# Scores as 64x64 quarters, q copied in one piece, the second batch's keys turned ahead of the MLP's second product

## The chip, the cores and the metric

The kernel runs on one core of a Trainium2 chip. The core has a matrix engine (TensorE, PE in the profile; its weight loads are listed as PEld), a vector engine (VectorE, DVE), an activation engine (ScalarE, ACT), a general engine (GpSimd, POOL) and a queue engine that issues DMAs (SyncE, SP). The metric is the device time in microseconds (us) of one execution. The time before is the median of three runs.

## The reference

Three stages follow each other. Everything is float32.

```python
# attention: q, k, v are (2, 8, 768, 64); block 32, window 16
k_sum = k.reshape(B, H, nb, block, D).max(axis=3)
v_sum = v.reshape(B, H, nb, block, D).mean(axis=3)
scores_l = where(|pos_q - pos_k| < window, scale * q @ k.T, -1e9)
scores_s = scale * q @ k_sum.T + log(block)
a = softmax(concat([scores_l, scores_s]))
x = a @ concat([v, v_sum])              # then to 1536 tokens x 512
# MLP: w_in (512, 2048), w_out (2048, 512)
h = x @ w_in;  x = (h * sigmoid(h)) @ w_out
# mixture of 8 experts, top 1, capacity 384: w1 (8, 512, 1024), w2 (8, 1024, 512)
e = argmax(x @ w_gate); out = gate * (relu(x @ w1[e]) @ w2[e])
```

## The kernel before

Attention works in 24 units. A unit is 256 queries (four blocks of 64) of a pair of heads; twelve units make a batch of the input, and four units with the same queries make one block `xT` of 256 tokens for the MLP. The main loop calls `attn_step(n)` for n from -2 on, and a step holds pieces of several units: the scores `s_mm` of unit n, the row minimum `s_max`, exponential `s_exp` and normalization `s_norm` of unit n-1, the turn of the probabilities `p_mm`/`p_ev` of unit n-2, the product with the values `a_mm` and its copies `x_hi`/`x_lo` of unit n-3, and the queries' turn `q_mm`/`q_ev` of unit n+1. From step 7 on a step also holds one MLP step s = n-7: `l1(s)`, twelve matmuls of 256 columns for one slice f of 128 hidden columns, `g_mul`, `g_hi`, `g_lo`, and `l2` of the step two before, six matmuls of 512 columns. There are 96 MLP steps; after the attention they go on alone, and the experts follow. The order in which the code calls the functions is the order on each engine; nothing is reordered later, and each engine works its instructions off one after the other.

The keys of a head pair are prepared by `k_prep(b, p)`: six transposes on PE into two PSUM banks kA and kB, copies by ACT of twelve overlapping windows of 96 keys into `kwin`, and the maxima of 32 keys by DVE (`ks`), which go behind each window as 24 more columns. A `k_prep` runs in steps -1 to 2 for the first batch and in steps 11 to 14 for the second one ("k steps" below), near the end of the step, after `l2`. The scores multiply a 128x128 stationary matrix `qbd`, in which the two heads' queries stand as a block diagonal (the rest is zero, set once by POOL), with the 120 columns of a window: four float32 matmuls for a unit, each of which the trace shows as two records. `q_ev` fills `qbd` by four ACT copies.

The block means of the values come in the first batch from PE (`vsum_mm`, six matmuls, called at the end of step 0; ACT copies the result), in the second batch from POOL and DVE (`vs_reduce`) with eight small DMAs (`vs_place`). `vs_rows` is the DMA that puts them under the values of each unit.

The MLP's weights W0, W1, ... are loaded raw as pairs `ri`, `ro` and turned into two float32r parts by `conv`: per half three DVE operations (`cv`), an ACT cast and a POOL subtraction. `conv_part` takes the next DVE operation of the queue, three of them in a step; `conv_until` forces what an `l1` needs. All attention tiles in PSUM share four buffers of the tag `att`.

## Time and profile before

| | |
|---|---|
| median of three runs | 515.15 us (514.3 to 515.69) |
| the profiled execution | 514.7 us, its span 513.0 us |
| busy share of the span | PE 94%, PEld 81%, DVE 58%, ACT 48%, POOL 26% |
| granted TensorE clock, mean | 0.976 of full speed |

The span runs from the first instruction to the last one in the trace. PE's share is an average: in the first four of 40 slices of the span the page shows it at 4 to 8 tenths, and in nearly all later ones at 9. A DVE, ACT or POOL that waits while PE is busy costs nothing.

### The profile page before, as it was taken

The page shows a single profiled execution, that of the slowest core. Times are in us where ns is not written, and L with a number is a line of the kernel's source. Part 1 is how long each engine was busy: PE and PEld are TensorE (multiplying, and loading weights), DVE is VectorE, ACT ScalarE, POOL GpSimd, SP SyncE. Part 2 cuts the span into 40 slices and gives each one's busy share as a digit, 9 for nine tenths or more (in the row PEclk, how much of TensorE's full clock was granted, in tenths as well). Part 3 has the DMA queues.
Part 4 walks back from the last instruction along what each step waited for, and adds up shares of the span by engine and source line. Part 5 has one row for each costly group of instructions (what it writes and reads, how often), then busy time and mean ns, then how long its engine had stood idle before and what let it go on. Part 6 is the DMA issues. An engine that isn't in the chain of part 4 may idle for free. (4 is left out here: it accounts for less than half of the span.)

```text
span 513.0 us, 9798 instructions
## 1 busy us (share of the span) xinstructions
PE 479.9 (94%) x3318; PEld 416.8 (81%) x3318; DVE 296.0 (58%) x857; ACT 247.4 (48%) x746; POOL 135.6 (26%) x154
## 2 busy tenths in 40 slices
PE   4877989999999999999999999999999998999994
PEld 2366878898988899999998998888878897988852
DVE  1277886765545988666666434556666673445500
ACT  4478868977753533333333333334543344346511
POOL 6027753362433532222112100112412012101011
PEclk9957989999999999999999999999999999999998
DMA  8479777246301677655540000128251367718470
GB/s 204 101 201 278 187 193 200 65 121 165 75 2 42 173 211 215 217 156 149 151 177 0 1 1 0 44 74 318 78 191 55 89 204 226 251 45 288 151 236 16
DMA packets 82055, 71.15 MB, mean 139 GB/s; under 512 B 36822, under 2 KB 66776, under 8 KB 81984
## 3 DMA queue, kind: packets, MB, share of 16 engines
q1 hardware_dynamic: 80288, 66.17, 44.6%
q0 software_dynamic: 1696, 4.13, 2.1%
q8 instruction: 33, 0.54, 0.4%
q14 instruction: 38, 0.31, 0.2%
HBM read 55.38 MB, written 15.09 MB: 137 GB/s over the span
## 5 line engine op out<-in xcount | busy, mean ns | idle before, releaser
L451 PE MATMUL hp<-xT,w 128*128 128x256 f32 x1152 | 156.8, 286 | 2.3 <-ACT w L436 1.4
L451 PEld LDWEIGHTS hp<-xT,w 128*128 128x128 f32 x1152 | 149.6, 192 | 8.1 <-ACT w L436 1.6
L481 PE MATMUL x<-w,g 128*128 128x512 f32 x576 | 151.6, 398 | 1.1 <-ACT rows L487 1.1
L481 PEld LDWEIGHTS x<-w,g 128*128 128x128 f32 x576 | 101.8, 189 | 20.2 <-issue 2.1
L454 ACT ACTIVATE u<-hp 128x256 f32<-128x256 f32 x96 | 37.0, 385 | 98.3 <-PE hp L451 94.8
L459 DVE SCALAR_TENSOR_TENSOR u<-u,hp 128x256 f32<-128x256 f32 x96 | 40.2, 418 | 63.9 <-ACT u L454 63.6
L463 ACT CAST g<-u 128x256 fp32r<-128x256 f32 x96 | 39.4, 410 | 60.3 <-DVE u L459 60.0
L437 POOL TENSOR_TENSOR w<-cv,w 128x512 fp32r<-128x512 f32 x32 | 42.8, 1339 | 95.9 <-ACT w L436 95.8
L791 PE MATMUL hp<-XT,H 128*128 128x384 f32 (+1 forms) x288 | 48.8, 320 | 2.2 <-ACTq L948 1.4
L791 PEld LDWEIGHTS hp<-XT,H 128*128 128x128 f32 x288 | 45.8, 188 | 4.6 <-ACTq L948 1.8
L757 PE MATMUL y<-H,gh 128*128 128x512 f32 x192 | 48.6, 397 | 0.0
L467 DVE TENSOR_TENSOR g<-u,g 128x256 fp32r<-128x256 f32 x72 | 31.4, 437 | 27.6 <-ACT g L463 17.0
L326 POOL TENSOR_TENSOR P<-P,rs 128x480 f32<-128x480 f32 x24 | 26.3, 1095 | 60.6 <-DVE rs L325 53.8
L757 PEld LDWEIGHTS y<-H,gh 128*128 128x128 f32 x192 | 35.1, 188 | 7.2 <-issue 0.4
L736 DVE TENSOR_TENSOR H<-R,H 128x1024 fp32r<-128x1024 f32 x24 | 29.4, 1224 | 17.2 <-ACT H L735 17.2
L568 POOL DMA_INDIRECT disp<-rows,di x12 | 13.4, 1119 | 97.5 <-DVE rows L566 58.7
L316 ACT ACTIVATE P<-P,nm 128x120 f32<-128x120 f32 x96 | 36.6, 384 | 4.2 <-DVE nm L305 4.1
L796 ACT ACTIVATE gh<-hp 128x384 fp32r<-128x384 f32 (+1 forms) x24 | 10.9, 456 | 47.2 <-PE hp L791 46.7
L294 PEld LDWEIGHTS sc<-kwin,qbd 128*128 128x128 f32 x192 | 28.3, 220 | 4.8 <-DVE nm L305 1.7
L294 PE MATMUL sc<-kwin,qbd 128*128 128x120 f32 x192 | 30.2, 308 | 2.0 <-DVE nm L305 1.0
L735 ACT CAST H<-R 128x1024 fp32r<-128x1024 f32 x27 | 28.1, 1042 | 2.2 <-SPq L948 1.6
L765 POOL DMA_INDIRECT out_dram<-ys,aux x8 | 9.8, 1231 | 72.2 <-ACT ys L764 36.5
(175 smaller groups left out, 576.7 us busy)
## 6 DMA issues: line engine op xcount, KB each, us to landing
R<-in_moe_w_dram SPq DMA_DIRECT2D x34, 512.0 KB
ri<-in_moe_w_in_dram SPq DMA_DIRECT2D x16, 512.0 KB
ro<-in_moe_w_out_dram SPq DMA_DIRECT2D x16, 512.0 KB
disp<-zt SPq DMA_DIRECT2D x24, 260.0 KB
q_n<-in_q_dram SPq DMA_DIRECT2D x48, 64.0 KB
k_n<-in_k_dram SPq DMA_DIRECT2D x16, 192.0 KB
out_dram<-zt SPq DMA_DIRECT2D x12, 256.0 KB
rows<-in_moe_w_dram SPq DMA_DIRECT2D x6, 512.0 KB
```

What stands on the lines that cost most here:

```text
L294: PE.matmul(sc[:, i, :], lhsT=qbd[u % 2][:, i, :], rhs=kwin[p][:, i0 + i, :], start=True, stop=True)
L316: ACT.activation(P[:, i, :], P[:, i, :], AF.Exp, bias=nm[:, i : i + 1], scale=-1.0, accum_out=sm[:, i : i + 1])
L437: POOL.tensor_sub(w[:, 2 * j + 1, :], t, w[:, 2 * j, :].bitcast(F32))
L451: PE.matmul(hp, lhsT=w[:, a, c], rhs=x[:, b_, kk, :], start=n == 0, stop=n == 3 * KT - 1)
L454: ACT.activation(u, hp, AF.Tanh, scale=0.5)
L459: DVE.scalar_tensor_tensor(out=u, in0=u, scalar=1.0, in1=hp_t.pop(s), op0=ALU.add, op1=ALU.mult)
L463: ACT.copy(gt[s][:, 0, :], u_t[s])
L467: eng.tensor_sub(gt[s][:, 1, :], u_t.pop(s), gt[s][:, 0, :].bitcast(F32))
L481: PE.matmul(x2[blk][t], lhsT=gh[:, a, c], rhs=w[:, b_, :], start=first and n == 0, stop=last and n == 2)
L736: (eng or DVE).tensor_sub(h[:, 1], r, h[:, 0].bitcast(F32))
L757: PE.matmul(y, lhsT=gh[:, a, c], rhs=mx[1, f // 2][:, b_, DM * (f % 2) : DM * (f % 2) + DM], start=first and n == 0, stop=last and n == 2,)
L791: PE.matmul(hp, lhsT=h1(f // 2, a, kk, c), rhs=XT[:, b_, kk, 0:N], start=n == 0, stop=n == 3 * KT - 1)
```

## The change

The scores: `qbd` is gone. `q_mm` turns the queries into a tile `qa` that stays allocated in one `att` buffer (its other half takes `a_mm`'s result), `q_ev` copies all 256 columns at once, and `s_mm` issues eight matmuls with a 64x64 stationary matrix: head h picks the rows of the array, the parity e of the query block its columns. Each head writes a PSUM tile of its own. The mask has three patterns instead of six. The q loads give each partition two pieces of 256 bytes, where it was one of 512.

The keys: kB takes seven instead of six transposes with kA together, so that no window is cut and four ACT copies do for eight. The first batch's kA and kB lie in the tag `x2`. The second batch's `k_prep` is called after `q_mm` and before `l2`.

The order: `vsum_mm` is called at the end of step 1 instead of 0, into the tag `h`, and DVE copies its result. `vs_rows` is called a step later (for unit n-2) and behind `l2`, `vs_place` a step later. W0 and W1 enter the conversion queue in steps 3 and 5 instead of 2 and 4. Constants that only the routing uses are made after the mask.

```diff
+    qa = psum.tile([128, 2, 256], F32, tag="att", bufs=4, name="qa")
...
-    mask = ap1.tile([128, 6, WK], F32, name="mask")
+
+    mask = ap1.tile([128, 3, WK], F32, name="mask")
     POOL.memset(mask, 0.0)
-    for h in range(2):
-        m = mask[64 * h : 64 * h + 64]
-        for lo, hi, off in ((0, 1, 0), (1, 5, WIN), (5, 6, 2 * WIN)):
+    for e, parts in enumerate((((0, 1, 0), (1, 3, WIN)), ((0, 2, WIN), (2, 3, 2 * WIN)))):
+        m = mask[QB * e : QB * e + QB]
+        for lo, hi, off in parts:
             for sgn in (1, -1):
 
                 POOL.affine_select(
@@ -124,9 +129,6 @@
     POOL.memset(mask[:, :, WL:WK], LOGB)
 
     kwin = [ap1.tile([128, NQB, WK], F32, name=f"kwin{p}") for p in range(NPAIR)]
-    qbd = [ap1.tile([128, UB, 128], F32, name=f"qbd{i}") for i in range(2)]
-    for t in qbd:
-        POOL.memset(t, 0.0)
...
...
+    def late_constants():
+        POOL.iota(iota_e, [[1, E]], base=0, channel_multiplier=0, allow_small_or_imprecise_dtypes=True)
+        POOL.memset(onesb, 1.0)
...
+    late_constants()
...
-            SP.dma_start(out=t[:, h], in_=q[b, 2 * p + h, s0 : s0 + TB, :].rearrange("(p r) d -> p r d", r=2))
+            SP.dma_start(out=t[:, :, h], in_=q[b, 2 * p + h, s0 : s0 + TB, :].rearrange("(t p) d -> p t d", p=128))
...
-        ps = psum.tile([128, H, D], F32, tag="att", bufs=4, name="vsp")
+        ps = psum.tile([128, H, D], F32, tag="h", bufs=2, name="vsp")
...
-        ACT.copy(vsum[WL:WK], ps[WL:WK])
+        DVE.tensor_copy(vsum[WL:WK], ps[WL:WK])
...
-        c0 = 512
-        pa = psum.tile([128, 512], F32, tag="att", bufs=4, name="kA")
-        pb = psum.tile([128, 512], F32, tag="att", bufs=4, name="kB")
-        for i in range(S // 128):
-            dst = pa[:, 128 * i : 128 * i + 128] if i < 4 else pb[:, 128 * i - 512 : 128 * i - 384]
-            PE.transpose(dst, t[:, i].rearrange("p h d -> p (h d)"), ident)
-        for src, lo, hi in ((pa, 0, c0), (pb, c0, S)):
-            i = 0
-            while i < NQB:
-                a, e = max(wstart(i), lo), min(wstart(i) + WL, hi)
-                if a >= e:
-                    i += 1
-                    continue
-                if e - a == WL:
-                    n = 1
-                    while i + n < NQB and wstart(i + n) == wstart(i) + n * QB and wstart(i + n) + WL <= hi:
-                        n += 1
-                    if n > 1:
-                        sl = src[:, a - lo : a - lo + 1]
-                        sap = bass.AP(tensor=sl.tensor, offset=sl.offset, ap=[list(sl.ap[0]), [QB, n], [1, WL]])
-                        ACT.copy(kw[:, i : i + n, 0:WL], sap)
-                        i += n
-                        continue
-                o = a - wstart(i)
-                ACT.copy(kw[:, i, o : o + e - a], src[:, a - lo : e - lo])
-                i += 1
+
+        parts = []
+        for name, lo, hi, w0, w1_, c in (("kA", 0, 512, 0, 7, 0), ("kB", 384, S, 7, NQB, 512)):
+
+            tag, bufs = ("x2", 2) if b == 0 else ("att", 4)
+            ps = psum.tile([128, 512], F32, tag=tag, bufs=bufs, name=name)
+            for i in range(lo // 128, hi // 128):
+                PE.transpose(ps[:, 128 * i - lo : 128 * i - lo + 128], t[:, i].rearrange("p h d -> p (h d)"), ident)
+            parts.append((ps, lo, hi, w0, w1_, c))
+        for ps, lo, hi, w0, w1_, c in parts:
+            i = w0
+            while i < w1_:
+                n = 1
+                while i + n < w1_ and wstart(i + n) == wstart(i) + n * QB:
+                    n += 1
+                a = wstart(i) - lo
+                assert a >= 0 and a + (n - 1) * QB + WL <= hi - lo
+                sl = ps[:, a : a + 1]
+                ACT.copy(
+                    kw[:, i : i + n, 0:WL],
+                    bass.AP(tensor=sl.tensor, offset=sl.offset, ap=[list(sl.ap[0]), [QB, n], [1, WL]]),
+                )
+                i += n
             DVE.reduce_max(
-                ks[:, lo // BLK : hi // BLK],
-                src[:, 0 : hi - lo].rearrange("p (n t) -> p n t", t=BLK),
+                ks[:, c // BLK : hi // BLK],
+                ps[:, c - lo : hi - lo].rearrange("p (n t) -> p n t", t=BLK),
                 axis=AX.X,
             )
         (POOL if b > 0 else DVE).tensor_copy(kw[:, :, WL:WK], ks.unsqueeze(1).to_broadcast([128, NQB, NSUM]))
...
     def q_mm(u):
-        qt = psum.tile([128, TB], F32, tag="att", bufs=4, name="qt")
+        qt = qa[:, 0]
         t = q_n.pop(u)
-        for h in range(2):
-            PE.transpose(qt[:, 128 * h : 128 * h + 128], t[:, h].rearrange("p r d -> p (r d)"), ident)
+        for i in range(2):
+            PE.transpose(qt[:, 128 * i : 128 * i + 128], t[:, i].rearrange("p h d -> p (h d)"), ident)
         qt_t[u] = qt
 
     def q_ev(u):
-        qt = qt_t.pop(u)
-        for h in range(2):
-            dst = qbd[u % 2][64 * h : 64 * h + 64, :, 64 * h : 64 * h + 64].rearrange("p i (c r) -> p i c r", r=2)
-            for r in range(2):
-
-                src = qt[64 * r : 64 * r + 64, 128 * h : 128 * h + 128]
-                ACT.copy(dst[:, :, :, r], src.rearrange("p (i c) -> p i c", c=QB // 2))
+        q_t[u] = ap2.tile([128, TB], F32, tag="qT", name="qT")
+        ACT.copy(q_t[u], qt_t.pop(u))
 
     def s_mm(u):
         T, p = divmod(u, NPAIR)
         i0 = (T % NTH) * UB
-        sc = psum.tile([128, UB, WK], F32, tag="att", bufs=4, name="sc")
-        for i in range(UB):
-            PE.matmul(sc[:, i, :], lhsT=qbd[u % 2][:, i, :], rhs=kwin[p][:, i0 + i, :], start=True, stop=True)
+
+        sc = [psum.tile([128, UB // 2, WK], F32, tag="att", bufs=4, name="sc") for _ in range(2)]
+        qT = q_t.pop(u)
+        for j in range(UB // 2):
+            for h in range(2):
+                w = slice(D * h, D * h + D)
+                for e in range(2):
+                    i = 2 * j + e
+                    PE.matmul(
+                        sc[h][QB * e : QB * e + QB, j, :],
+                        lhsT=qT[w, QB * i : QB * i + QB],
+                        rhs=kwin[p][w, i0 + i, :],
+                        start=True,
+                        stop=True,
+                    )
         sc_t[u] = sc
 
     def s_max(u):
         i0 = (u // NPAIR % NTH) * UB
-        m0 = 0 if i0 == 0 else (2 if i0 + UB == NQB else 1)
         P = ap2.tile([128, UB, WK], F32, tag="P", name="P")
 
         sc = sc_t.pop(u)
         nm = ap2.tile([128, UB], F32, tag="nm", name="nm")
-        for i in range(UB):
+        for g in range(UB):
+            h, j = divmod(g, UB // 2)
+            i = i0 + 2 * j
             DVE.tensor_tensor_reduce(
-                out=P[:, i, :], in0=sc[:, i, :], in1=mask[:, m0 + i, :], scale=-scale, scalar=3.0e38,
-                op0=ALU.add, op1=ALU.min, accum_out=nm[:, i : i + 1],
+                out=P[:, g, :], in0=sc[h][:, j, :], in1=mask[:, 0 if i == 0 else 2 if i == NQB - 2 else 1, :],
+                scale=-scale, scalar=3.0e38, op0=ALU.add, op1=ALU.min, accum_out=nm[:, g : g + 1],
             )
...
-        av = psum.tile([128, TB], F32, tag="att", bufs=4, name="av")
+        av = qa[:, 1]
         for i in range(UB):
             for h in range(2):
                 PE.matmul(
                     av[64 * h : 64 * h + 64, QB * i : QB * i + QB],
                     lhsT=vt[0:WK, i, h, :],
-                    rhs=ps[0:WK, i, 64 * h : 64 * h + 64],
+                    rhs=ps[0:WK, UB // 2 * h + i // 2, QB * (i % 2) : QB * (i % 2) + QB],
...
-        if n > 1 and (n - 1) % NPB == 0 and n - 1 < NU:
+        if n > 2 and (n - 2) % NPB == 0 and n - 2 < NU:
             vs_place()
         on(p_mm, n - 2)
         conv_part()
         on(g_mul, s, NS)
         on(load_v, n - 1)
-        on(vs_rows, n - 1)
         on(s_exp, n - 1)
         conv_part()
         on(q_mm, n + 1)
         on(x_hi, n - 3)
-        if n == 0:
-            for T in range(NTH):
-                load_vp(0, T)
+        b, r = divmod(n + 1, NPB)
+        if 0 < b < B and r < NPAIR:
+
+            k_prep(b, r)
         l2_to(s - 2)
+        on(vs_rows, n - 2)
         on(p_ev, n - 2)
         on(q_ev, n + 1)
         on(s_norm, n - 1)
@@ -1076,7 +1085,7 @@
             vs_reduce(b, r)
         on(x_lo, n - 3)
         b, r = divmod(n + 1, NPB)
-        if 0 <= b < B and r < NPAIR:
+        if b == 0 and r < NPAIR:
             k_prep(b, r)
         on(g_hi, s, NS)
         if n in (4, 5):
@@ -1088,6 +1097,9 @@
         on(g_lo, s, NS)
         on(s_mm, n)
         if n == 0:
+            for T in range(NTH):
+                load_vp(0, T)
+        if n == 1:
             vsum_mm(0)
 
     NS = len(steps)
@@ -1096,7 +1108,7 @@
     for n in range(-2, NS + 2 + LEAD):
         s = n - LEAD
         if s < 0:
-            if n in (2, 4):
+            if n in (3, 5):
                 conv_to(n // 2)
             attn_step(n)
             continue
```

On PE at the start of the program, before the change: the keys of the second pair (step 0), the scores of unit 0, the block means `vsp`, then the queries and keys of the next units, the scores of unit 1 and the first probabilities.

```order
L242 MATMUL kA<-ident,k_n 128x128 x4
L242 MATMUL kB<-ident,k_n 128x128 x2
L294 MATMUL sc<-kwin_144,qbd_148 128x120 x4
L207 MATMUL vsp<-vp_n,avg 24x512 x6
L277 MATMUL qt<-ident,q_n 128x128 x2
L242 MATMUL kA<-ident,k_n 128x128 x4
L242 MATMUL kB<-ident,k_n 128x128 x2
L294 MATMUL sc<-kwin_145,qbd_149 128x120 x4
L332 MATMUL pt<-ident,P 120x128 x4
```

The same place of the changed kernel:

```order
L247 MATMUL kA<-ident,k_n 128x128 x4
L247 MATMUL kB<-ident,k_n 128x128 x3
L295 MATMUL sc<-kwin_126,qT 64x120 x8
L277 MATMUL qa<-ident,q_n 128x128 x2
L247 MATMUL kA<-ident,k_n 128x128 x4
L247 MATMUL kB<-ident,k_n 128x128 x3
L295 MATMUL sc<-kwin_127,qT 64x120 x8
L210 MATMUL vsp<-vp_n,avg 24x512 x6
L340 MATMUL pt<-ident,P 120x128 x4
```

The six matmuls of `vsp` have moved behind the next unit's queries, keys and scores, right ahead of the first `pt`.

On PE in a k step (step 11), from `l1` to the scores, before the change:

```order
L451 MATMUL hp<-xT,w 128x256 x12
L356 MATMUL av<-PT,v_n 64x64 x8
L332 MATMUL pt<-ident,P 120x128 x4
L277 MATMUL qt<-ident,q_n 128x128 x2
L481 MATMUL x_875<-w,g 128x512 x3
L481 MATMUL x_876<-w,g 128x512 x3
L242 MATMUL kA<-ident,k_n 128x128 x4
L242 MATMUL kB<-ident,k_n 128x128 x2
L294 MATMUL sc<-kwin_147,qbd_149 128x120 x4
```

And in the changed kernel:

```order
L459 MATMUL hp<-xT,w 128x256 x12
L364 MATMUL qa<-PT,v_n 64x64 x8
L340 MATMUL pt<-ident,P 120x128 x4
L277 MATMUL qa<-ident,q_n 128x128 x2
L247 MATMUL kA<-ident,k_n 128x128 x4
L247 MATMUL kB<-ident,k_n 128x128 x3
L489 MATMUL x_1260<-w,g 128x512 x3
L489 MATMUL x_1261<-w,g 128x512 x3
L295 MATMUL sc<-kwin_127,qT 64x120 x8
```

The keys' transposes stand ahead of `l2` (the rows that write x) instead of behind it. In the changed kernel the two PSUM banks of sc are also those of kA and kB in such a step.

On DVE in a k step, before the change, from `g_mul` (it writes u) to the maxima `ks`:

```order
L459 SCALAR_TENSOR_TENSOR u<-u,hp 128x256
L338 COPY PT<-pt 120x512
L324 TENSOR_SCALAR rs<-sm 128x4
L325 RECIPROCAL rs<-rs 128x4
L374 TENSOR_TENSOR xT<-av,xT 128x256
L263 TENSOR_REDUCE ks<-kA 128x16
L263 TENSOR_REDUCE ks<-kB 128x8
```

And in the changed kernel:

```order
L467 SCALAR_TENSOR_TENSOR u<-u,hp 128x256
L263 TENSOR_REDUCE ks<-kA 128x16
L263 TENSOR_REDUCE ks<-kB 128x8
L346 COPY PT<-pt 120x512
L332 TENSOR_SCALAR rs<-sm 128x4
L333 RECIPROCAL rs<-rs 128x4
L382 TENSOR_TENSOR xT<-qa,xT 128x256
```

The two maxima have moved from the end to the place behind `g_mul`.

## Rows read from the trace of the kernel before

**Rows 1.** Windows: length; busy PE, PEld, DVE, ACT, POOL (xinstructions); clock; DMA; GB/s.

```profile
21.00:50.40 29.40, 20.91 (x157) 17.79 (x157) 19.81 (x72) 24.74 (x100) 14.07 (x15) 0.73 0.80 216
50.40:74.40 24.00, 20.90 (x183) 18.47 (x182) 20.79 (x69) 17.59 (x67) 14.51 (x16) 0.90 0.76 193
74.40:98.40 24.00, 23.86 (x219) 21.19 (x218) 15.79 (x63) 21.09 (x94) 8.98 (x12) 1.00 0.59 143
98.40:144.80 46.40, 46.17 (x433) 41.83 (x432) 28.09 (x125) 34.80 (x144) 18.71 (x21) 1.00 0.45 108
144.80:480.00 335.20, 330.66 (x2119) 294.90 (x2119) 201.96 (x499) 134.45 (x305) 67.55 (x57) 1.00 0.42 132
```

**Rows 2.** Timeline of PE, 0 to 51 us: start, length, instruction [idle before, releaser].

```profile
9.48 1.11 PE L242 MATMUL kA<-ident,k_n 128*128 128x128 f32 x4 [1.80 <-ACT qbd L287]
...
11.98 2.03 PE L294 MATMUL sc<-kwin,qbd 128*128 128x120 f32 x8
13.95 7.07 PE L207 MATMUL vsp<-vp_n,avg 128*24 128x512 f32 x12
...
21.96 1.05 PE L294 MATMUL sc<-kwin,qbd 128*128 128x120 f32 x8
...
29.23 2.06 PE L294 MATMUL sc<-kwin,qbd 128*128 128x120 f32 x8 [0.82 <-ACT PT L338]
...
50.44 2.19 PE L451 MATMUL hp<-xT,w 128*128 128x256 f32 x12
```

**Rows 3.** Timeline of ACT at the start.

```profile
8.29 1.14 ACT L287 COPY qbd<-qt 64x128 f32<-64x128 f32 x4 [2.83 <-POOL qbd L129]
...
21.05 0.58 ACT L211 COPY vsum<-vsp 24x512 f32<-24x512 f32 x1 [7.46 <-PE vsp L207]
```

**Rows 4.** Timelines of DVE and POOL at 49 us.

```profile
49.16 1.50 DVE L324 TENSOR_SCALAR rs<-sm 128x4 f32<-128x4 f32 x1 [1.08 <-ACT P L316]
...
49.37 1.26 POOL L437 TENSOR_TENSOR w<-cv,w 128x512 fp32r<-128x512 f32 x1
```

**Rows 5.** Timeline of PE, `l1` of step 10.

```profile
66.63 0.50 PE L451 MATMUL hp<-xT,w 128*128 128x256 f32 x2 [1.41 <-ACT w L436]
67.98 1.95 PE L451 MATMUL hp<-xT,w 128*128 128x256 f32 x10 [0.84 <-POOL w L437]
```

**Rows 6.** Timeline of PE, a whole step without `k_prep`.

```profile
119.36 1.68 PE L451 MATMUL hp<-xT,w 128*128 128x256 f32 x12
120.96 0.69 PE L356 MATMUL av<-PT,v_n 120*64 120x64 f32 x16
121.58 0.65 PE L332 MATMUL pt<-ident,P 128*120 128x128 f32 x4
122.07 0.38 PE L277 MATMUL qt<-ident,q_n 128*128 128x128 f32 x2
122.20 1.62 PE L481 MATMUL x<-w,g 128*128 128x512 f32 x6
123.67 1.05 PE L294 MATMUL sc<-kwin,qbd 128*128 128x120 f32 x8
124.47 0.72 PE L451 MATMUL hp<-xT,w 128*128 128x256 f32 x4
```

**Rows 7.** Experts' matmuls on alternating column halves: ns min/median/max, first and last start, shape.

```profile
L837 PE MATMUL hp<-R,few x32: 379/379/401, 488.0 to 491.5; 128*64 128x256 f32 x32
```

**Rows 8.** Timelines of ACT and DVE: query and key copies, maxima.

```profile
123.17 1.12 ACT L287 COPY qbd<-qt 64x128 f32<-64x128 f32 x4
...
92.11 0.24 ACT L261 COPY kwin<-kA 128x96 f32<-128x96 f32 x1
92.25 0.65 ACT L257 COPY kwin<-kA 128x576 f32<-128x576 f32 x1
...
87.93 0.69 DVE L263 TENSOR_REDUCE ks<-kA 128x16 f32<-128x512 f32 x1 [2.55 <-ACT kwin L261]
```

**Rows 9.** Timeline of SP, the eight DMAs of `vs_place`.

```profile
89.63 6.20 SPq L231 DMA_DIRECT2D vsum<-vs_t  x8
```

More of the change, by code (lines that the diff above doesn't have):

```diff
@@ L78 @@
     iota_e = const.tile([128, E], F32, name="iota_e")
-    POOL.iota(iota_e, [[1, E]], base=0, channel_multiplier=0, allow_small_or_imprecise_dtypes=True)
     onesb = const.tile([128, 128], BF16, name="onesb")
-    POOL.memset(onesb, 1.0)
     utri = const.tile([128, 128], BF16, name="utri")
-    POOL.affine_select(
-        out=utri, in_=onesb, pattern=[[1, 128]], compare_op=ALU.is_gt, fill=0.0, base=0, channel_multiplier=-1
-    )
     iota_s = const.tile([128, E], F32, name="iota_s")
-    POOL.iota(iota_s, [[1, E]], base=1, channel_multiplier=0, allow_small_or_imprecise_dtypes=True)
     crun = const.tile([128, E], BF16, name="crun")
-    POOL.memset(crun, 0.0)
     rows = const.tile([128, NTT, RW], F32, name="rows")
     tok = rows.bitcast(I32)[:, :, DM + 1 : DM + 2]
-    POOL.memset(rows[:, :, DM + 2 :], 0.0)
-    POOL.iota(tok.rearrange("p t o -> p (t o)"), [[128, NTT]], base=0, channel_multiplier=1)
+    def late_constants():
+        POOL.iota(iota_e, [[1, E]], base=0, channel_multiplier=0, allow_small_or_imprecise_dtypes=True)
+        POOL.memset(onesb, 1.0)
+        POOL.affine_select(
+            out=utri, in_=onesb, pattern=[[1, 128]], compare_op=ALU.is_gt, fill=0.0, base=0, channel_multiplier=-1
+        )
+        POOL.iota(iota_s, [[1, E]], base=1, channel_multiplier=0, allow_small_or_imprecise_dtypes=True)
+        POOL.memset(crun, 0.0)
+        POOL.memset(rows[:, :, DM + 2 :], 0.0)
+        POOL.iota(tok.rearrange("p t o -> p (t o)"), [[128, NTT]], base=0, channel_multiplier=1)
     big = ctx.enter_context(tc.tile_pool(name="big", bufs=GROUPS[0] + 1 + NBLK))
@@ L270 @@
     xT = {}
-    qt_t, sc_t, p_t, st_t, pp_t, pt_t, av_t = {}, {}, {}, {}, {}, {}, {}
+    qt_t, q_t, sc_t, p_t, st_t, pp_t, pt_t, av_t = {}, {}, {}, {}, {}, {}, {}, {}
     def q_mm(u):
-        qt = psum.tile([128, TB], F32, tag="att", bufs=4, name="qt")
+        qt = qa[:, 0]
         t = q_n.pop(u)
-        for h in range(2):
-            PE.transpose(qt[:, 128 * h : 128 * h + 128], t[:, h].rearrange("p r d -> p (r d)"), ident)
+        for i in range(2):
+            PE.transpose(qt[:, 128 * i : 128 * i + 128], t[:, i].rearrange("p h d -> p (h d)"), ident)
         qt_t[u] = qt
     def q_ev(u):
-        qt = qt_t.pop(u)
-        for h in range(2):
-            dst = qbd[u % 2][64 * h : 64 * h + 64, :, 64 * h : 64 * h + 64].rearrange("p i (c r) -> p i c r", r=2)
-            for r in range(2):
-                src = qt[64 * r : 64 * r + 64, 128 * h : 128 * h + 128]
-                ACT.copy(dst[:, :, :, r], src.rearrange("p (i c) -> p i c", c=QB // 2))
+        q_t[u] = ap2.tile([128, TB], F32, tag="qT", name="qT")
+        ACT.copy(q_t[u], qt_t.pop(u))
     def s_mm(u):
@@ L291, in s_mm @@
         i0 = (T % NTH) * UB
-        sc = psum.tile([128, UB, WK], F32, tag="att", bufs=4, name="sc")
-        for i in range(UB):
-            PE.matmul(sc[:, i, :], lhsT=qbd[u % 2][:, i, :], rhs=kwin[p][:, i0 + i, :], start=True, stop=True)
+        sc = [psum.tile([128, UB // 2, WK], F32, tag="att", bufs=4, name="sc") for _ in range(2)]
[11 more added lines that the diff above has]
+                        stop=True,
+                    )
         sc_t[u] = sc
```

## The prediction

> **What bounds the kernel now.** I read the windows first, cut where the trace changes its character [rows 1]. From 98.4 us on PE is the bound: 46.17 of 46.40 us with attention and MLP together, 330.66 of 335.20 us after that. There 1 us of PE more or less in a step is 1 us of time, and what ACT saves is worth nothing. From 74.4 to 98.4 us (the four k steps) PE is still nearly full. Ahead of 74.4 us it is not: from 21.0 to 50.4 us ACT has the most work (24.74 of 29.40 us) and the granted clock is 0.73; from 50.4 to 74.4 us DVE has it (20.79 of 24.00 us). So the change has two accounts: what it shortens before 74.4 us, which moves everything behind it forward, and what it does to PE's own steps after.
>
> The timelines show what the first stretch waits for. PE's block means take from 13.95 to about 21.0 us; the scores of unit 1 come at 21.96, those of unit 2 only at 29.23, the first `l1` at 50.44 [rows 2]. ACT stood for 7.46 us in the copy of the block means, with the exponentials of unit 0 queued behind it, and at the start 2.83 us for POOL, which was filling `qbd` [rows 3]. PE's fourth `l1` waits 1.41 and 0.84 us for W3 [rows 5], which hangs on DVE's conversions.
>
> **The change, part by part.** *Start.* The 2.83 us for `qbd` go; the first ACT copy of queries falls from four pieces (1.14 us) to one. Against that stand a seventh transpose and q loads in shorter pieces. PE waited 1.80 us for ACT before the second keys [rows 2]. I take the scores of unit 0 as 2.0 us earlier (bounds 1.0 and 2.8).
>
> *Block means later.* Now the next queries, keys and the scores of unit 1 stand ahead of them. At the slow clock this is 2 + 7 transposes of about 0.23 us (from 1.11 us for four, less the overlap at the end, [rows 2]) and scores of 1.9 us, together 3.9 us. The means themselves ran 7.07 us, 0.59 us for each of twelve records of equal size; more PE work ahead of them should bring the clock up before them, which I value at 1.7 us (0 to 2). They end at 21.0 - 2.0 + 3.9 - 1.7 = 21.2 us, as before. But meanwhile ACT, freed from their copy, does the exponentials of unit 0 and the keys of pair 2, and POOL the normalization. After the means PE has only `pt`, `qa` and seven transposes (some 1.7 us) ahead of the scores of unit 2, and DVE the copy of the means (0.58 us on ACT, [rows 3]) and `s_max`: scores of unit 2 at about 23.0 instead of 29.23 us. **-6.2 us**; bounds -3 (DMAs of keys and values late) and -8.
>
> *Steps 3 to 6.* ACT loses 0.75 us a step: four query copies take 1.12 us, one of 256 columns about 0.37, between the 0.24 us for 96 and 0.65 us for 576 [rows 8]. But POOL and DVE hold each other in these steps: a DVE operation on four columns takes 1.50 us while POOL subtracts a weight for 1.26 us [rows 4], and POOL's work is the same. Of some 3 us I take **-0.6 us** (0 to -3).
>
> *W0 and W1 a step later.* W1's second half now ends in step 7, in front of W2 and W3, on which PE waits [rows 5]. **+0.4 us** (0 to +2.5). The shared bank `qa` makes `a_mm` wait for the last `x_lo`, which is late on DVE in steps 8 and 9; PE's idle time before W3 covers it, and without that cover it costs about 1 us. With this the first account is -6.4 us.
>
> *Scores.* In a plain step the scores take from 123.67 to 124.47, 0.80 us for eight records [rows 6]. Now they are sixteen of the same 120 columns on quarters. How these overlap is read from two places. The experts' matmuls alternate between two column halves: the first of 32 records starts at 488.0, the last at 491.5 us, so two records per 0.22 us for 256 columns [rows 7]. `av` does the same with 64 columns: 0.62 us for sixteen records [rows 6], where eight pairs at a quarter of 0.22 make 0.44. Two at a time is what a matmul in two records allows when records start in order: the second one has the same quarter as the first and must follow it, the next matmul's first one runs beside it. For 120 columns a pair is 0.103 us; eight pairs 0.82, one half pair alone 0.10, and what `av` shows beyond its pairs and its half pair, 0.62 - 0.44 - 0.05 = 0.13, for going into and out of the form: 1.05 us, +0.25 a step. It counts in the 14 steps 10 to 23: **+3.5 us**; the bounds are those of the two rivals on the quarters, -2.2 and +13.7.
>
> This 0.13 us in `av` is the row that speaks against the change. [...] Without this cost the scores would take 0.92 us, and the term would be +1.7 us. [...]
>
> *k steps.* One transpose more, 0.1 us each (six take 0.62 us, [rows 6]). The maxima now gate the scores, since kA and kB lie in their banks. After the start of `l1` (119.36), ACT comes to the query copies 3.8 us later (123.17, [rows 8]); there the copies of kA now stand, 0.8 us, then DVE's maximum 0.69 us: 5.3 us; kB's about 5.7 us. PE has `l1` to `qa` (2.84 us), seven transposes (0.7) and `l2` (1.47), 5.0 us, and 0.1 for the form [rows 6, 8]. It waits about 0.3 us. The old k step also waited: 24.0 us for four [rows 1], where the plain 5.11 and six transposes make 5.7. So four steps cost 4 x (0.1 + 0.3) less 4 x 0.2 that they waited already, **+0.8 us** (-0.5 to +3, where `vs_reduce` comes in between).
>
> *At no cost*, with their cover: the mask in halves and the later constants (POOL is done long before the first normalization); DVE's copy of the means, priced above; fewer copies of keys after 74.4 us (ACT is not the bound); `vs_rows` behind `l2`, since the values are wanted in the next step, 1.6 us after its start. `vs_place` holds SP for 6.20 us [rows 9] and now stands ahead of the loads of unit 13 and the rows of unit 12; were they late, PE would wait 1 to 3 us once.
>
> **Sum.** -6.2 - 0.6 + 0.4 + 3.5 + 0.8 = -2.1 us against the profiled execution's own 514.7 us: 512.6. That execution lies 0.45 us under the median of 515.15, so I predict 513.0 us; the rivals below are set against the median too.
>
> **Rivals.** *Quarters one at a time.* If records on quarters of different rows don't overlap as column halves do, the scores take 16 x 0.103 + 0.13 = 1.78 us, +0.98 a step, +13.7 us instead of +3.5: 523.3 us, slower. Nothing in the trace has row halves, so it is open; against it speak the pairs of rows 7 and of `av`. It decides from a cost of 0.4 us a step on (6.4 - 0.8 over 14). *Four at a time.* Then 4 x 0.103 + 0.10 + 0.13 = 0.64 us, -0.16 a step, -2.2 us: 507.3 us. Against it: in rows 7 two column halves, each with both records of a matmul behind one another, never got beyond two records in 0.22 us. [...] *The start gives less.* If DVE's conversions or the DMAs, with 0.76 to 0.80 busy share [rows 1], bound W3 whatever the start does, only some 3 us of the 6.4 arrive: +1.3, 516.5 us, slower. For it speaks DVE's 20.79 of 24 us; against it that the raw weights need no PE. *The start gives more.* If ACT was the bound in steps 3 to 6 after all (24.74 of 29.40 us), its whole 3 us arrive and the sum is -4.5: 510.6 us.
>
> **Numbers.** A difference of 0.3% (1.5 us) is about what a measurement can tell from none. The forecast 0.52, its own range 510.8 to 515.5; quarters one at a time 0.08; four at a time 0.08; start less 0.20; start more 0.12. Faster by over 0.3%, under 513.6: 0.3 of the forecast's part, 0.12 and 0.08, 0.50. Slower, over 516.7: 0.03 of the forecast's part, 0.08, and 0.13 of the start's: 0.24. Same: 0.26. The range from 508.5 to 517.5 leaves out the two cases of the quarters and the end of the third.
>
> **What would show it.** Right: scores of unit 2 near 23 us and the first `l1` near 44; a plain step of about 5.4 instead of 5.11 us, with the scores' sixteen records in about 1.05 us; k steps near 6.5 us with PE waiting for DVE's maxima. Wrong: scores of 0.64 or 1.8 us; PE waiting for `qa`, for `v_n` or longer for W3; the first `l1` near 44 and the fifth still near 74.

## The result, and the profile after

The changed kernel takes 521.88 us (median of 4 runs, 521.09 to 523.56), the kernel before 514.75 us beside it: ratio 1.0148, 95% interval 1.0119 to 1.0177. The forecast was 513.0. The profiled execution has a span of 519.3 us, where before it was 513.0.

PE's timeline at the start of the changed kernel answers to [rows 2].

```profile
10.62 1.08 PE L295 MATMUL sc<-kwin,qT 64*64 64x120 f32 x16
...
14.68 5.41 PE L210 MATMUL vsp<-vp_n,avg 128*24 128x512 f32 x12
...
21.93 0.64 PE L295 MATMUL sc<-kwin,qT 64*64 64x120 f32 x16
...
31.03 1.12 PE L364 MATMUL qa<-PT,v_n 120*64 120x64 f32 x16 [3.84 <-DVE xT L382]
...
37.84 1.12 PE L364 MATMUL qa<-PT,v_n 120*64 120x64 f32 x16 [3.21 <-DVE xT L382]
...
46.57 2.63 PE L459 MATMUL hp<-xT,w 128*128 128x256 f32 x12
```

The scores of unit 2 come at 21.93 us (23.0 was forecast), but the first `l1` only at 46.57 (44): twice `a_mm` waits over 3 us for `x_lo`. A plain step, beside [rows 6]:

```profile
123.61 1.70 PE L459 MATMUL hp<-xT,w 128*128 128x256 f32 x12
...
125.24 0.69 PE L364 MATMUL qa<-PT,v_n 120*64 120x64 f32 x16
...
126.48 1.63 PE L489 MATMUL x<-w,g 128*128 128x512 f32 x6
128.04 0.64 PE L295 MATMUL sc<-kwin,qT 64*64 64x120 f32 x16
128.61 1.70 PE L459 MATMUL hp<-xT,w 128*128 128x256 f32 x12
```

The step takes 128.61 - 123.61 = 5.00 us where it took 5.11. The sixteen records of the scores take 0.57 us, not the 0.80 of before and not the 1.05 of the forecast: a third of sixteen times 0.103 us. From `l2` to the scores it is 1.56 us instead of 1.47, and from `l1` to the values' product 1.63 instead of 1.60: of the 0.13 us forecast for going into and out of the form, 0.09 stand at the way in and 0.03 at the way out. In and behind the k steps PE waits in other places:

```profile
76.61 0.96 PE L295 MATMUL sc<-kwin,qT 64*64 64x120 f32 x16
77.49 1.69 PE L459 MATMUL hp<-xT,w 128*128 128x256 f32 x12
...
80.05 0.69 PE L364 MATMUL qa<-PT,v_n 120*64 120x64 f32 x16 [0.86 <-DVE xT L382]
...
100.22 0.69 PE L364 MATMUL qa<-PT,v_n 120*64 120x64 f32 x16 [1.50 <-DMA v_n<-vsum]
```

All this is small. The loss stands in the experts, whose code the change doesn't touch. The kernel before, PE's timeline behind the first expert class:

```profile
457.89 4.46 PE L757 MATMUL y<-H,gh 128*128 128x512 f32 x18
463.17 3.09 PE L791 MATMUL hp<-XT,H 128*128 128x256 f32 x24 [0.82 <-ACTq L959]
...
487.98 3.86 PE L837 MATMUL hp<-R,few 128*64 128x256 f32 x32 [1.09 <-ACTq L959]
```

The same three places of the changed kernel:

```profile
457.62 4.46 PE L765 MATMUL y<-H,gh 128*128 128x512 f32 x18
464.78 4.63 PE L799 MATMUL hp<-XT,H 128*128 128x256 f32 x24 [2.70 <-ACTq L967]
...
492.73 5.22 PE L845 MATMUL hp<-R,few 128*64 128x256 f32 x32 [2.71 <-ACTq L967]
```

At 457.62 us the changed kernel is still 0.27 us ahead. At 464.78 it is 1.61 behind, at 492.73 it is 4.75 behind, at the end 6.3. L967 is a `tc.If`: a branch of ACT's program. PE idles 1.9 and 1.6 us longer, and the 24 and 32 matmuls behind each idle time take 1.5 and 1.4 us longer. The windows say why these matmuls take longer (length, busy PE, PEld, DVE, ACT, POOL, clock, DMA, GB/s), behind the first branch, first of the changed kernel, then of the kernel before:

```profile
465.00:468.40 3.40, 3.40 (x18) 3.40 (x18) 1.57 (x2) 1.81 (x3) 0.75 (x1) 0.52 1.00 320
```

```profile
463.20:466.60 3.40, 3.40 (x27) 3.27 (x28) 1.78 (x3) 2.62 (x4) 0.22 (x1) 1.00 0.81 224
```

Behind the longer idle time the granted clock is 0.52 in its window; before the change it is 1.00. Behind the second branch it is 0.55 from 492.80 to 496.20 us, where before the change it is 1.00 from 488.00 to 491.40. ACT's and DVE's own first instructions behind the branch, of the changed kernel:

```profile
465.33 1.04 ACT L743 CAST H<-R 128x1024 fp32r<-128x1024 f32 x1 [2.54 <-ACTq L967]
...
462.43 0.17 DVE L784 COPY aux<-Xg 128x4 f32<-128x4 f32 x1 [2.90 <-DVEq L967]
```

and of the kernel before:

```profile
463.73 1.05 ACT L735 CAST H<-R 128x1024 fp32r<-128x1024 f32 x1 [0.65 <-ACTq L959]
...
460.50 0.17 DVE L776 COPY aux<-Xg 128x4 f32<-128x4 f32 x1 [0.70 <-DVEq L959]
```

No data is late there; the engine's own queue is. The DMA view of the changed kernel from ACT's branch to its next instruction (462.2 to 464.7 us) has, for q14, one of the two queues that the page calls `instruction`:

```profile
q14 instruction: 2, 0.02, 2.5%
```

The same view before the change, 462.46 to 463.10 us, has none:

```profile
DMA packets 0, 0.00 MB, mean 0 GB/s; under 512 B 0, under 2 KB 0, under 8 KB 0
```

Theory A from here on: at the branch the engine waits for its code to be fetched, and where the code lies decides whether it must wait. The change shortens ACT's program ahead of the experts by 115 instructions and lengthens DVE's by 19 (counted in the built programs), so everything behind lies elsewhere. The rival (B): work or data of the changed kernel arrive later.

### The profile page after: what moved, and what is told of

The parts are those of the page before. It is cut to its first block, busy times and chain, and to the rows that moved or that the text cites. A ratio compares the mean times of both kernels' runs of the same rounds, so it can differ in the third digit from the quotient of the medians.

```text
span 519.3 us, 10124 instructions
## 1 busy us (share of the span) xinstructions
PE 477.8 (92%) x3518; PEld 408.4 (79%) x3518; DVE 299.2 (58%) x858; ACT 225.8 (43%) x641; POOL 130.7 (25%) x148
## 5 line engine op out<-in xcount | busy, mean ns | idle before, releaser
L459 PE MATMUL hp<-xT,w 128*128 128x256 f32 x1152 | 158.4, 287 | 0.3 <-POOL w L445 0.3
L799 PE MATMUL hp<-XT,H 128*128 128x384 f32 (+1 forms) x288 | 50.3, 327 | 4.1 <-ACTq L967 2.7
L799 PEld LDWEIGHTS hp<-XT,H 128*128 128x128 f32 x288 | 47.3, 196 | 6.6 <-ACTq L967 3.1
L475 DVE TENSOR_TENSOR g<-u,g 128x256 fp32r<-128x256 f32 x72 | 34.0, 472 | 27.6 <-ACT g L471 16.5
L364 PE MATMUL qa<-PT,v_n 120*64 120x64 f32 x384 | 18.2, 244 | 15.7 <-DVE xT L382 10.9
L364 PEld LDWEIGHTS qa<-PT,v_n 120*64 120x64 f32 x384 | 14.8, 152 | 19.8 <-DVE xT L382 11.9
L773 POOL DMA_INDIRECT out_dram<-ys,aux x8 | 8.0, 997 | 75.6 <-ACT ys L772 52.8
```

What stands on the lines that cost most here:

```text
L364: PE.matmul(av[64 * h : 64 * h + 64, QB * i : QB * i + QB], lhsT=vt[0:WK, i, h, :], rhs=ps[0:WK, UB // 2 * h + i // 2, QB * (i % 2) : QB * ...
L459: PE.matmul(hp, lhsT=w[:, a, c], rhs=x[:, b_, kk, :], start=n == 0, stop=n == 3 * KT - 1)
L475: eng.tensor_sub(gt[s][:, 1, :], u_t.pop(s), gt[s][:, 0, :].bitcast(F32))
L799: PE.matmul(hp, lhsT=h1(f // 2, a, kk, c), rhs=XT[:, b_, kk, 0:N], start=n == 0, stop=n == 3 * KT - 1)
```

## Experiments

Positions are compared in steps of 128 instructions. The 128 are the author's assumption. On the page of the changed kernel the queue's row (packets, MB) gives 8 KB a packet; no run shows what a packet holds.

```profile
q14 instruction: 40, 0.32, 0.2%
```

**Instructions added that are executed (e1, e2).** To the kernel before, as many on ACT and DVE as shift the code by 13 and 19; to the changed one, as many as bring it back.

```diff
     def mlp_step(s):
+        if steps[min(s, NS - 1)][0] in (1, 2) and s < NS:
+            for k, eng in ((0, ACT), (1, DVE)):
+                for _ in range(min(4, pads[k])):
+                    pads[k] -= 1
+                    (ACT.copy if k == 0 else DVE.tensor_copy)((padA, padD)[k][:, 0:1], ident[0:1, 0:1])
```

> The kernel before, with one-element copies added in the MLP steps of the second and third weight group, where both engines have room: 16 on ACT (its code after them moves by 13 instructions) and 19 on DVE (by 19). These are the shifts of the changed kernel, up to 128 instructions. Theory A (code position): the 6.4 us are lost in the experts because ACT and DVE wait for their code behind two branches, and where the code lies decides that. It expects the same two waits here: ACT some 2.6 us behind the branch where it was 0.7, PE idle 2.7 us before each of the two, its clock lower after them, and 520 to 522 us. Theory B (the changed work or its data arrive later): nothing of the work has changed here, so 514.3 to 515.7 us as before.

> The changed kernel, with one-element copies in the same MLP steps: 152 on ACT, after which its code lies where it lay before the change, and 109 on DVE, 128 instructions off. Theory A: the waits behind the branches are 0.7 us again and PE idles 0.8 and 1.1 us there; 521.9 less 6.4 is 515.5 us, or up to 1 us less where PE's lead of 1.3 us from the first 350 us is kept. Theory B: 521 to 523.5 us.

The edit of e2 has 153 copies on ACT.

e1: 522.88 us, ratio 1.0182 (1.0148 to 1.0216). e2: 523.56, 1.0184 (1.0158 to 1.0209). PE behind the branches, e1 and then e2:

```profile
465.44 4.63 PE L794 MATMUL hp<-XT,H 128*128 128x256 f32 x24 [2.65 <-ACTq L962]
```

```profile
471.06 3.14 PE L802 MATMUL hp<-XT,H 128*128 128x256 f32 x24 [0.82 <-ACTq L970]
```

Both waits moved as theory A said, and so did those at the second branch (2.59 us in e1, 1.15 in e2). e2's time didn't, because the copies were not free: four on each engine delayed `u` and `g`, and PE waited. Its 42nd `l1` starts 7.8 us later than that of the changed kernel. e1 paid 2.7 us in the same steps. So neither time decides.

**Later hints (e3, e4).** The kernel calls `mark_branch_hint_location` ahead of a branch, with a list of engines; here the call for ACT and DVE comes later.

```diff
-                tc.mark_branch_hint_location(*skip, engines=[PE.engine])
-            if half == 0 and f == 2 and skip is not None:
-                tc.mark_branch_hint_location(*skip, engines=[ACT.engine, DVE.engine])
+                tc.mark_branch_hint_location(*skip, engines=[PE.engine, ACT.engine, DVE.engine])
```

> The changed kernel with the branch hints of ACT and DVE four loop turns later, where that of PE already stands; no other edit. Theory A: fewer instructions between hint and branch leave less room for what goes wrong there; if the hint is what is lost, ACT and DVE run on after 0.7 us and the time is 514 to 515.5 us. If the position matters but not through the hint, 521 to 523. Theory B: 521 to 523.5 us.

> The kernel before with the same later hints. Theory A: its waits behind the branches are short already, so 514.3 to 515.7 us; and this is the base for parts of the change that are tried alone. Theory B: the same.

e3: 522.64 us, 1.0170 (1.0145 to 1.0196): the waits stay (2.63 and 2.62 us). e4: 516.55, 1.0078 (1.0046 to 1.0111), not the same as before. Its PE rows:

```profile
462.30 3.12 PE L791 MATMUL hp<-XT,H 128*128 128x256 f32 x24 [0.82 <-ACTq L957]
...
488.61 3.74 PE L837 MATMUL hp<-R,few 128*64 128x256 f32 x32 [2.59 <-ACTq L957]
```

The place of the call does matter, at the second branch: with the later one PE idles 2.59 us there instead of 1.09, though the call still stands two turns of the loop ahead of its end. Both theories had expected no change.

**Instructions added that are never executed (e5, e6).** They stand in the other arm of a branch that isn't taken.

```diff
     with cmp.Else():
         rq.extend([route(NBLK - 1), tables()])
         route_all()
         second_few(0)
+        for i in range(115):
+            ACT.copy(pad[0][:, 0:1], ident[0:1, 0:1])
+        for i in range(109):
+            DVE.tensor_copy(pad[1][:, 0:1], ident[0:1, 0:1])
```

> The changed kernel; in the branch of the program that is never taken (the first expert not full) stand 115 more copies on ACT and 109 on DVE. Nothing more is executed; the code behind them lies where it lay before the change, in steps of 128 instructions. Theory A (code position): no long wait behind the branches, the experts take 50.6 us from ACT's branch to the end of the span as before the change, not 57.2: 521.9 less some 6.5 us, 514.5 to 516 us. Theory B (the work or its data arrive later): 521 to 523.5 us.

> The kernel before, with 13 copies on ACT and 19 on DVE in the branch that is never taken: not one executed instruction differs. Theory A: ACT and DVE wait some 2.5 and 3 us behind both branches, 520 to 522 us. Theory B: the time of before, 513 to 516 us.

e5: 516.65 us, ratio 1.0067 (1.0040 to 1.0093). e6: 521.44, 1.0147 (1.0112 to 1.0182). PE, e5 and then e6:

```profile
463.91 3.12 PE L800 MATMUL hp<-XT,H 128*128 128x256 f32 x24 [0.82 <-ACTq L968]
...
488.80 3.77 PE L846 MATMUL hp<-R,few 128*64 128x256 f32 x32 [1.20 <-ACTq L968]
```

```profile
465.28 4.25 PE L792 MATMUL hp<-XT,H 128*128 128x256 f32 x24 [2.78 <-ACTq L960]
...
493.08 5.43 PE L838 MATMUL hp<-R,few 128*64 128x256 f32 x32 [2.60 <-ACTq L960]
```

This decides for A. Not one executed instruction of e6 differs from the kernel before, and it has the changed kernel's loss and its waits; the changed kernel with its code put back is rid of these waits, and of most of its loss. B falls; but e5 lies 0.65 us over the range of theory A, and only ACT's and DVE's code was put back, not that of PE, POOL and SP. The traces agree with one another here: from the 18 `y` matmuls ahead of the first branch to the end of the span it is 55.1 us before the change and 55.2 in e5, but 61.7 in the changed kernel and 61.5 in e6.

**Which engine (e14, e15).** The same edit on the kernel before, 13 copies on ACT alone, 19 on DVE alone.

> The kernel before with 13 copies on ACT in the branch that is never taken, none on DVE. If ACT is what PE waits for (in the changed kernel ACT comes back 2.6 us after its branch, DVE 3 us after a branch that it reaches 3.5 us earlier), PE idles 2.7 us at both branches and the time is 520 to 522 us. If DVE alone holds PE, 513 to 516.

> The kernel before with 19 copies on DVE in the branch that is never taken, none on ACT. If ACT is what PE waits for, DVE's late return (some 2 us) is hidden behind PE's second product: 513 to 516 us. If DVE holds PE too, over 517.

e14: 522.6 us, 1.0150 (1.0104 to 1.0197), 0.6 over the range expected. e15: 515.08, 1.0001 (0.9972 to 1.0031). The timelines of PE, ACT and DVE, e14 and then e15:

```profile
462.64 4.50 PE L792 MATMUL hp<-XT,H 128*128 128x256 f32 x24 [2.60 <-ACTq L960]
463.19 1.05 ACT L736 CAST H<-R 128x1024 fp32r<-128x1024 f32 x1 [2.43 <-ACTq L960]
458.20 0.17 DVE L777 COPY aux<-Xg 128x4 f32<-128x4 f32 x1 [0.69 <-DVEq L960]
...
490.74 6.53 PE L838 MATMUL hp<-R,few 128*64 128x256 f32 x32 [3.08 <-ACTq L960]
```

```profile
462.91 3.12 PE L792 MATMUL hp<-XT,H 128*128 128x256 f32 x24 [0.82 <-ACTq L960]
463.47 1.05 ACT L736 CAST H<-R 128x1024 fp32r<-128x1024 f32 x1 [0.65 <-ACTq L960]
462.17 0.22 DVE L777 COPY aux<-Xg 128x4 f32<-128x4 f32 x1 [2.62 <-DVEq L960]
```

ACT's wait is the whole loss. DVE comes to its branch earlier (in e14 it goes on at 458.20 us, ACT at 463.19), so its wait is hidden. From the `y` matmuls to the end it is 62.8 us in e14 and 55.0 in e15. The DMA view of e14 from ACT's branch to its next instruction (460.08 to 462.57 us) has one packet of q14:

```profile
q14 instruction: 1, 0.01, 0.9%
```

So the runs show that the place of ACT's code decides the wait. That the wait is the fetch itself is argued from these packets and was not tested. That 13 instructions more do here what 115 fewer do in the changed kernel agrees with the step of 128; no other step was tried.

**The quarters alone (e7).** The code is that of the change for `q_mm`, `q_ev`, `s_mm`, `s_max`, the mask and the q loads, with `qt` and `av` in buffers of their own. In this run and the following ones, never-executed copies keep the code's position.

> The kernel before with the quarters alone (queries in one copy, eight 64x64 matmuls in two PSUM banks, the mask in halves, `qbd` gone); keys, means, order and conversions as before; its code behind the never-taken branch brought to the old place. In the changed kernel a plain step fell from 5.11 to 5.00 us. Theory C: the quarters are that gain, 0.1 us in each of 14 steps, and the two banks leave the shared PSUM buffers enough room: 1.5 to 4 us faster than before (with 2.8 us of POOL's fill of `qbd` at the start). Theory D: five tiles a step in four buffers make PE wait for the previous readers: same or up to 5 us slower.

515.01 us, 1.0009 (0.9986 to 1.0031): no difference, as theory D allows; the gain of theory C isn't there. In its trace PE leads by 1.3 us at the end of attention, which is less than equal work differs by (last table of this section), and loses 0.6 in one step of routing. The scores of both heads in one PSUM bank were not tried.

**The change's own waits (e8 to e13).** e8 gives the first units' product a bank of its own:

```diff
-        av = qa[:, 1]
+        av = psum.tile([128, TB], F32, tag="x2", bufs=2, name="av") if u < 6 else qa[:, 1]
```

> The changed kernel at the old code position, with the values' product of the first six units in the two PSUM banks that the MLP does not yet use, in place of the shared `qa`. In the changed kernel PE waited 10.9 us, four times, ahead of that product for `x_lo` on DVE. Theory E: this wait is the shared bank's; it goes, the first `l1` comes 3 to 6 us earlier and the fifth 2 us earlier; 512 to 514 us. Theory F: DVE is late anyway (20.8 of 24 us before the change), so PE waits for it at the scores or the probabilities instead: within 1 us of the run with the old code position alone.

516.02 us, 1.0045 (1.0026 to 1.0064). That is within 1 us of e5, as theory F said. The waits for `x_lo` fall from 10.9 to 0.9 us, and others take a part of their place (the waits of PE, 0 to 110 us: sum, times, longest):

```profile
PE av L365 <- DMA v_n<-vsum: 4.6, 2, 2.8
...
PE av L365 <- ACT w L445: 2.1, 1, 2.1
PE av L365 <- DVE ks L264: 2.0, 1, 2.0
```

The next three runs start from e8, with `vs_place` in step 13; e10 has `vsum_mm` in step 0 besides, e11 W0 and W1 in steps 2 and 4.

```diff
-        if n > 2 and (n - 2) % NPB == 0 and n - 2 < NU:
+        if n > 1 and (n - 1) % NPB == 0 and n - 1 < NU:
             vs_place()
```

> The changed kernel at the old code position, the first six units' value products in the free banks (as in the run before), and `vs_place` a step earlier again, where it was before the change. Theory G: in the changed kernel the eight small DMAs stand on SP right ahead of the rows of unit 12, so PE waits 1.2 to 3.8 us for `v_n` in step 15 (1.5 in the run before this); the wait goes, and the step from the eighth to the ninth `l1` is 1 to 3 us shorter: 513 to 515 us. Theory H: the rows would have come late anyway, since they are now called behind `l2`: no change, 516 us.

> As the run with `vs_place` earlier, with the block means in step 0 again (still in the tag h, copied by DVE). Theory I (the term of 6.2 us for later means): the scores of unit 2 come later than 21.9 us, up to 26, and the first `l1` 3 to 5 us later than 45.3 us. Theory J: with ACT relieved of the copy and of `qbd`, the place of the means matters little: scores of unit 2 within 1.5 us, the first `l1` within 1.5 us.

> As the run with `vs_place` earlier, with W0 and W1 in the conversion queue in steps 2 and 4 again. Theory K (the 0.4 us term): W3 is ready 0.3 to 2 us earlier, so the fourth and fifth `l1` come up to 1 us earlier; the time within 0.3%. Theory L: the conversions on DVE in step 2 hold up the probabilities of the first units, and the first `l1` comes 0.5 to 2 us later.

Here unit 11 gets the means of the second batch, so the routing is another one; the times (574.41, 576.44 and 574.79 us) say nothing, and only the stretch ahead of the experts is read. In e9 the rows of unit 11, forgotten under both theories, stand behind the eight DMAs, and PE waits 4.38 us for them in step 14: neither theory is decided. With the means in step 0 (e10) the scores of unit 2 come at 29.56 us, with the means in step 1 (e9) at 21.63, but by the table below that is worth only 2.9 us at the first `l1` and 3.8 at the fifth: theory I, though the scores come later than its 26 us and the first `l1` just misses its 3. The later conversions, for which a loss of 0.4 us was forecast, show a gain of 1.4 us at the first `l1` and 0.6 at the fifth (e9 against e11). The sign is that of theory L, but equal work differs by as much, so it isn't shown.

e12 calls the rows first in a step and `vs_place` behind those of unit 11; e13 leaves them behind `l2`, with `vs_place` right after.

```diff
+        on(vs_rows, n - 2)
+        if n > 1 and (n - 1) % NPB == 0 and n - 1 < NU:
+            vs_place()
         on(load_q, n + 2)
```

> The changed kernel at the old code position, the first six units' value products in the free banks, and on SP the rows of unit n-2 first in a step, ahead of the queries and values; `vs_place` stands behind the rows of unit 11 (a step earlier than in the change, and right this time: the three runs before gave unit 11 the means of the second batch). Theory G: the waits for `v_n` (2.8 and 1.8 us in steps 4 and 5, 1.2 to 3.8 in step 15) go; the ninth `l1` lies 3 to 5 us ahead of the kernel before, a lead of 3 to 4 us stays up to the experts, and the time is 511 to 513.5 us, faster than before. Theory H: DVE and ACT, not the rows, end these waits: 514.5 to 516 us.

> The changed kernel at the old code position, the first six units' value products in the free banks, and `vs_place` right behind the rows of unit 11 in step 13, a step earlier than in the change; the rows stay behind `l2`. Theory G: the wait for `v_n` in step 15 goes and nothing takes its place; the ninth and tenth `l1` keep a lead of 2.5 us or more, and the time is 513 to 514.5 us, at or under the kernel before. Theory H: the eight DMAs then hold the queries of unit 15 or the values of unit 13, and a wait of 1 us or more stands in step 14 or 15 again: 515 to 516.5 us.

e12: 519.20 us, 1.0095 (1.0061 to 1.0129). e13: 516.75, 1.0025 (0.9994 to 1.0057). In e12 the waits for `v_n` fall from 6.5 us in e8 to 0.8, as theory G said, but one wait for POOL's probabilities takes 5.38 us and in step 14 the queries come 1.33 us late, behind the eight DMAs; the time lies over the ranges of both theories. In e13 the eight DMAs start 0.36 us earlier than in e8 (88.17 instead of 88.53 us), and PE still waits 2.10 us in step 15; the matmuls behind this wait run at a granted clock of 0.66 (100.00 to 104.80 us), so the step costs 3.3 us of lead. That is theory H, 0.25 us over its range.

PE's lead over the kernel before, in us, as the difference of the starts of an `l1`:

| kernel | 1st | 5th | 9th | 10th | 24th | 96th |
|---|---|---|---|---|---|---|
| the change | 3.9 | 3.1 | 1.3 | 0.2 | 1.3 | 0.3 |
| e3, the same work | 4.7 | 5.0 | 2.2 | -1.6 | -0.5 | -1.3 |
| e5, the same work, code in place | 3.8 | 3.0 | 0.2 | -0.3 | 0.9 | 0.0 |
| e7, quarters alone | 2.2 | 1.9 | 0.9 | 0.2 | 1.3 | 0.4 |
| e8, own bank | 5.2 | 4.3 | 2.5 | 1.0 | 2.1 | 1.3 |
| e9, unit 11 late | 5.5 | 5.2 | -4.1 | -3.7 | -2.6 | -3.6 |
| e10, means early | 2.6 | 1.3 | -6.1 | -5.7 | -4.6 | -5.5 |
| e11, conversions early | 4.1 | 4.6 | -3.9 | -3.4 | -2.3 | -3.4 |
| e12, rows first | 2.8 | 1.3 | -1.8 | -1.4 | -0.3 | -1.1 |
| e13, `vs_place` behind the rows | 5.4 | 4.9 | 2.2 | -1.1 | 0.0 | -0.9 |
| e4, e6, e14, e15: the work of the kernel before | -0.1 to 2.0 | 0.5 to 1.8 | -0.3 to 2.3 | 0.0 to 2.5 | 0.2 to 2.7 | 0.2 to 2.7 |

The last row shows how far a single trace can be trusted. In these four runs the same instructions are executed up to the experts as in the kernel before, and still their leads spread over 1.4 to 2.6 us at each place; of the five traces of this work that of the kernel before is the latest or the latest but one. So the gain of the change at the first `l1` is real (3.8 to 4.7 us against 2.0 at most), but at the 24th no lead is left (-0.5 to 1.3 against 0.0 to 2.7), and a difference of 1 or 2 us between two rows shows nothing by itself.

No version was faster than the kernel before beyond its interval.

## Why the prediction was wrong

*The step that failed* is the one that closed the account: "From 98.4 us on PE is the bound [...] and what ACT saves is worth nothing", and a sum whose last term is the k steps. What ACT saves in instructions moved its code behind the branches, and there it costs 6.6 us (from 0.27 ahead at 457.62 us to 6.3 behind at the end): 3.5 us of longer idle time of PE, 2.9 us of slower matmuls at the lower clock (0.52 and 0.55), 0.2 behind them. No term of the sum stood for the experts, and no rival had it. The rival of 523.3 us lies near the result, but its mechanism is not there; its nearness is luck.

*Scores*: the term was +3.5 us, from two records at a time. What was mis-sized is the overlap: the records take 0.57 us instead of 0.92. Going into and out of the form costs 0.12 us, about the 0.13 forecast. Together that is 0.69, against the 0.64 of the rival with four at a time, and a plain step gains 0.11 us, -1.5 us over 14 steps. That rival's mechanism fits: the 0.57 us lie nearer to four at a time (0.51) than to two (0.92). [rows 7] were a poor witness: they have halves of the columns, not quarters.

*Start*: -6.4 us was forecast, 3.1 us arrived at the fifth `l1` (3.0 and 5.0 in e5 and e3). The scores of unit 2 came 1.1 us earlier than forecast, the first `l1` 2.6 us later, so later means are worth less than the 6.2 us of the sum (2.9 to 3.8 by e9 and e10). The means themselves ran 5.41 instead of 7.07 us, the 1.7 us of the forecast: before the change the longest of their records takes 1.06 us and the median 0.59, in the changed kernel none takes more than 0.61. That the clock did it is not shown, for the granted clock reads 1.00 during the means in both traces. What took a part of the gain was named, but for steps 8 and 9 alone, and priced at nothing: `a_mm` waits for `x_lo` through the shared bank, without cover. PE's waits up to 110 us, and DVE's timeline ahead of the second one:

```profile
PE qa L364 <- DVE xT L382: 10.9, 4, 3.8
```

```profile
35.42 0.43 DVE L430 TENSOR_SCALAR cv<-ro 128x512 uint32<-128x512 uint32 x1 [3.64 <-DMA ro<-in_moe_w_out_dram]
...
37.37 0.42 DVE L382 TENSOR_TENSOR xT<-qa,xT 128x256 fp32r<-128x256 f32 x1
```

The copy `x_lo` (37.37 us) stands behind a conversion that waits 3.64 us for raw weights, so PE waits with it. With a bank of its own (e8, e9, e13, which change nothing else that early) the first `l1` leads by 5.2 to 5.5 us instead of 3.8 to 4.7, the fifth by 4.3 to 5.2 instead of 3.0 to 5.0: other waits take most of the place. The size is that of the rival "the start gives less"; which of the waits holds the fifth `l1` was not separated.

*k steps*: 1.8 us lost from the fifth to the ninth `l1`, as the terms +0.8 and four times +0.25 said; in e3 and e5 it is 2.8, so the hit is partly luck. Three of the four steps take 6.3 us, one 7.0, behind the wait of 0.86 us for `x_lo`. The gain of the scores isn't there in such a step: they take 0.88 us (76.61 to 77.49), as in the kernel before (85.53 to 86.41). The old k step's own waiting, 6.0 - 5.7 = 0.3 us, was counted as 0.2.

*At no cost*: PE waits 1.50 us for the rows behind `vs_place` in step 15, inside the 1 to 3 us named as the price without cover. The cover wasn't there, and in e9, e12 and e13 moving `vs_place` only moved the wait: some 6.4 us of SP in a step of 5 to 6 us push something back.

So without the accident of the code the change is no gain either: e5 is slower by 0.4 to 0.9%. Some 0.8 us of that stand in routing: from the 24th to the 96th `l1` every trace with the changed scores loses 0.8 to 1.1 us, and those of e4, e6, e14 and e15 lose nothing. The medians lie 2.7 us apart (516.65 and 513.99), the spans of the two traces only 0.8: the execution traced for e5 took 515.51 us, 1.1 less than its median, that of the kernel before 514.7, 0.7 more than its median. So where 1.9 of the 2.7 us go stays open. A part may be step 15, which cost 1.2 us in the trace of the change and 3.8 in that of e3, where PE waited 2.61 us and then ran at a granted clock of 0.67 (100.00 to 104.00 us).

## What to carry to other kernels

A change that adds or removes instructions ahead of a run-time branch moves the code behind it; here 13 copies that never ran cost 1.5% (e14). Look at the first instruction behind each branch in the trace, and compare with copies in an arm that never runs, before the difference in time is put down to the work. Such a copy also tells how much two traces of the same work differ; a lead of 1 or 2 us is read only against that. A small operation that stands on its engine behind one that waits for a transfer inherits the wait, and a shared buffer hands it on: here DVE's copy of 0.42 us stood behind a conversion that waited 3.64 us, and PE waited 3.21 us for the copy. Look also for a run of DMA issues on one queue that takes longer than a step: here, with some 6.4 us in steps of 5 to 6 us, it pushed something back where it stood, and three other places only moved the wait.
